# Eleven operand instructions an item on GpSimd in place of VectorE, in a gated scan with two feed-forward layers

## The chip, the cores and the metric

The kernel runs on one core of one Trainium2 chip. The core has a matrix engine (PE, with its weight loads as PEld), a vector engine (VectorE, DVE), an activation engine (ScalarE, ACT), a general engine (GpSimd, POOL) and a queue that issues DMAs (SyncE, SP). Each works through its own list of instructions in order; they meet through semaphores. The metric is the time of one execution on the device in microseconds, as a median over runs.

## The reference

A gated scan over 6080 steps and two batches gives 12160 tokens of 256 values. Two feed-forward layers follow, each 256 to 2048 to 256, with different activations.

```python
sig = 1.0 / (1.0 + np.exp(-f_logit))
f = lower_bound + (1.0 - lower_bound) * sig
for t in range(S):                       # h, y: [B, 256]
    h = f[:, t] * h + (1 - f[:, t]) * x[:, t]
    y[:, t] = h
x = y.reshape(B * S, D)                  # 12160 x 256
h = x @ w_in1;  x = (h - np.tanh(h)) @ w_out1
h = x @ w_in2;  x = np.maximum(0.01 * h, h) @ w_out2
```

All is float32. The kernel keeps that precision by splitting each matmul operand in two parts, a high half that the matrix engine takes as it is (fp32r) and a low half, the rest: a product is then three matmuls, high x high, low x high and high x low.

## The kernel before, in words

**Items.** The tokens are cut in 12 blocks of 1024 (the last has 896), and a block passes through each layer as one *item*. The list of items alternates: item 0 and 1 are blocks 0 and 1 of layer one, then second-layer and first-layer items take turns (item 2 is block 0 of layer two, item 3 block 2 of layer one, and so on); from item 3 on, odd items are first-layer ones up to item 21, even items second-layer ones, and item 23 is the second-layer item of the last block. An item has 8 *units* of 256 of the 2048 inner values; a unit has four quarter steps (the calls of `work`).

**Products.** From item 3 on a unit computes its four 128 x 512 blocks c11, c12, c21, c22 by a scheme of seven products in place of eight (`product`), so it needs seven operands made of the four quarters of the token block: three quarters as they are (B11, B21, B22) and four differences, T1 to T4. Each has a high and a low half, in the tiles xh and xl of the item (two buffers of each, by `forms`). `make_forms` makes the jobs that write them: `split_hi` casts on ACT (line 570), `sub` takes a difference into a slot of the ring "t" (line 578), `split_lo` subtracts the high half from the value (line 574). The differences hang together: T2 is B22 minus T1, T4 is B21 minus T2. For a second-layer item the quarters come from the tile z, the result of layer one; for a first-layer item from y, the result of the scan.

**The rest of a unit.** ACT applies the activation (lines 658, 660); in layer one DVE subtracts it from the value (`shrink`, line 666); ACT casts the high half (`hi`, line 685) and DVE makes the low half (`lo`, line 690); `emit_B` (line 729) multiplies both by the second weight into four accumulator banks. Lines 1280 and 1324 on DVE add a copy (`s5`) to a PSUM bank of PE; line 1324 writes to an SBUF tile c22, line 1280 to the bank c12. Lines 779 and 791 join partial sums of the second-layer item before (`drain`, `combine`), line 824 transposes its output blocks, which SP then stores.

**What sets the order.** The order is written by hand: a table `side` says which jobs are called at which quarter step, and each job's instructions go to the end of its engine's list at the call. The operands of the next item are made during the item before it. In a first-layer item the jobs of the next second-layer item's operands come first, mixed with the output jobs of the item before, then the scan of the block for the next first-layer item:

```python
at = base + (10 if full else 6 if it == W0 - 1 else 4)
lay(base + 5, at, forms_in[:11 if full else 0])
rest_in = mix(forms_in[11 if full else 0:], outs)
```

`lay` spreads jobs over quarter steps by their weights; `base` is the first quarter step of the item, and `full` holds for items 7, 9, ... 21. So eleven of the eighteen jobs (six of them low halves and differences) are called within quarter steps 5 to 10. The order of the jobs there is: high halves of B11, B21, B22; low half of B11; T1; low half of B21; high half of T1; low half of B22; T3; low half of T1; high half of T3; then T2, low half of T3, high half of T2, T4, low half of T2, high half and low half of T4. In items 3 and 22 the jobs are spread over nearly the whole item, one or a few at a time.

Of the kernel before, what the change touches and what calls it, by code (L numbers as in the profile page):

```python
# [8 lines left out]
F32 = mybir.dt.float32  # L9
# [5 lines left out]
ALU = mybir.AluOpType  # L15
# [5 lines left out]
def tile_gated_scan_two_ffn(  # L21
# [23 lines left out]
    nc = tc.nc  # L45
# [15 lines left out]
    NPLAIN = 3  # L61
# [48 lines left out]
    def light(f, w=0.4):  # L110
        weight[f] = w
        return f
# [438 lines left out]
    def make_forms(it, spread=False):  # L551

        l, c = items[it]
        h = macros[c][1] // 2
        s = {}

        def q(k, n):
            if l == 0:
                return ys[c][:, k, n * h:(n + 1) * h]
            return zs[c][:, k, n, :h]  # L560

        def get(i):
            if i in s:
                return s[i][:, :h]
            return {B11: q(0, 0), B21: q(1, 0), B22: q(1, 1), B12: q(0, 1)}[i]

        def split_hi(i):
            if it not in forms:
                forms[it] = [xp.tile([P, 7, H], F32R, tag=f"x{v}", name=f"x{v}") for v in "hl"]
            nc.scalar.copy(forms[it][0][:, i, :h], get(i))  # L570

        def split_lo(i):
            hi, lo = forms[it]
            nc.vector.tensor_tensor(lo[:, i, :h], get(i), hi[:, i, :h].bitcast(F32), ALU.subtract)

        def sub(i, a, b):
            s[i] = sp.tile([P, H], F32, tag="t", bufs=6, name="t")
            nc.vector.tensor_tensor(s[i][:, :h], a(), b(), ALU.subtract)

        if it < NPLAIN:  # L580
            return [f for i in (B11, B21, B12, B22) for f in (
                lambda i=i: split_hi(i), lambda i=i: split_lo(i)
            )]
        jobs = []
        for i, make in (
            (B11, None), (B21, None), (B22, None),
            (T1, lambda: sub(T1, lambda: q(0, 1), lambda: q(0, 0))),
            (T3, lambda: sub(T3, lambda: q(1, 1), lambda: q(0, 1))),
            (T2, lambda: sub(T2, lambda: q(1, 1), lambda: get(T1))),
            (T4, lambda: sub(T4, lambda: q(1, 0), lambda: get(T2))),  # L590
        ):
            if make:
                jobs.append(make)
            jobs += [light(lambda i=i: split_hi(i)), lambda i=i: split_lo(i)]
        if spread:
            first = (0, 2, 4, 1, 6, 3, 7, 5, 9) if l else (0, 2, 1, 4, 3, 6, 5, 7, 9)
            jobs = [jobs[i] for i in first + (8, 10, 12, 11, 13, 15, 14, 16, 17)]
        return jobs
# [313 lines left out]
    with tc.manual_schedule():  # L912
# [105 lines left out]
        for u, (load, jobs, _) in enumerate(w):  # L1018
            a = begin[NU - 1] + 3 + 43 * u // 8
# [3 lines left out]
        a = 2 * I + 18  # L1023
# [54 lines left out]
        for it in range(2, len(items) - 1):  # L1078
            base = I * it
            l, c = items[it + 1]  # L1080
            if it in outer:
                f, w = make_forms(it + 1, True), crossing[it]
                a = 7 if l == 0 else 0
# [114 lines left out]
        for t in range(NPLAIN * NU, NC):  # L1198
# [4 lines left out]
            it, v = divmod(t, NU)  # L1203
            grp = []
            if it in outer and 2 <= v < crossing[it] + 2 or v < 2 and crossing.get(it - 1) == NU:
                a, w = (it, v) if v > 1 else (it - 1, v + NU)
                g, i = divmod(w - 2, 2)
                pairs[a, g] = us_of[a][2 * g:2 * g + 2]
                grp = [(a, g, 2 * i), (a, g, 2 * i + 1)]
            if t < NC:  # L1210
# [3 lines left out]
                b1, h = u["b1"], u["h"]  # L1214
# [102 lines left out]
            if it in outer and v < crossing[it]:  # L1317
                g, i = divmod(v, 2)
# [58 lines left out]
```

## Time and profile before

| | |
|---|---|
| median of 3 runs | 1936.88 us (1936.64 to 1938.4) |
| profiled execution | span 1935.1 us from its first to its last instruction; the median of the runs, which counts what lies around the span too, is 1.8 us more |
| PE busy | 1927.7 us, 100% by the page |
| DVE busy | 1748.6 us, 90% |
| ACT busy | 1496.7 us, 77% |
| POOL busy | 3.3 us, 11 instructions, the last before 19 us |
| PE clock | granted in full in all 40 slices |

The page's first part gives busy time by engine over the whole span. The table of stretches (`windows` of the trace) gives the same for parts of it, so it tells where an engine has room. The timeline gives instructions one by one with their start; a row can merge several of one kind, and then its duration is from the first's start to the last's end. Consecutive instructions of an engine overlap a little, so the spacing of starts is shorter than a duration.

### The profile page before, as it was taken

How to read it: one execution, taken by the hardware profiler on the slowest of the kernel's cores; microseconds unless marked ns; L12 is line 12 of the kernel's file. 1: busy time of each engine (PE TensorE's matmuls, PEld its weight loads, DVE VectorE, ACT ScalarE, POOL GpSimd, SP SyncE). 2: the span in 40 equal slices, each digit the busy share in tenths (PEclk: the TensorE clock that was granted, in tenths of full speed). 3: DMA queues.
4: the chain of work that ended last, by engine and by line, in shares of the span. 5: the costliest groups of instructions: out<-in, count | busy, mean ns of one | idle time of the engine just before them, and what ended most of it. 6: DMA issues, size and time to landing. Idle time of an engine off the chain costs nothing.

```text
span 1935.1 us, 26099 instructions
## 1 busy us (share of the span) xinstructions
PE 1927.7 (100%) x8606; PEld 1607.2 (83%) x8606; DVE 1748.6 (90%) x2848; ACT 1496.7 (77%) x2773; POOL 3.3 (0%) x11
## 2 busy tenths in 40 slices
PE   9999999999999999999999999999999999999999
PEld 7888888888888888888888888888888888889888
DVE  8989879878899988999999999999899999987997
ACT  7556656766698689689779769868968977976997
POOL 0000000000000000000000000000000000000000
PEclk9999999999999999999999999999999999999999
DMA  6668678987575757757567476575765756646665
GB/s 218 181 154 282 232 255 299 261 274 241 169 206 175 191 187 202 182 182 216 151 185 214 150 196 194 190 182 194 204 170 176 215 147 193 192 161 187 211 198 139
DMA packets 478214, 384.86 MB, mean 199 GB/s; under 512 B 280960, under 2 KB 367872, under 8 KB 478080
## 3 DMA queue, kind: packets, MB, share of 16 engines
q1 hardware_dynamic: 477568, 382.98, 66.0%
q8 instruction: 68, 1.11, 0.2%
q14 instruction: 66, 0.54, 0.1%
q10 hardware_dynamic: 512, 0.23, 0.0%
HBM read 341.31 MB, written 41.81 MB: 198 GB/s over the span
## 4 chain that ended last, share of the span: by engine, by line
PE 98%; DVE 1%; DMA 0%; issue 0%; ACT 0%; SPq 0%
PE acc L729 30%; PE b L606 23%; PE c L606 18%; PE acc L768 11%; PE acc L746 8%; PE b L628 5%; PE c L729 1%; PE c L628 1%; DMA rawx<-in_x_dram 0%; DVE g L666 0%; DVE gl L690 0%; PE b L636 0%; PE b L614 0%; DVE y L478 0%; SPq L445 0%
## 5 line engine op out<-in xcount | busy, mean ns | idle before, releaser
L729 PE MATMUL acc<-gh,wb 128*128 128x512 f32 (+1 forms) x1760 | 595.2, 387 | 0.0
L690 DVE TENSOR_TENSOR gl<-g,gh 128x512 fp32r<-128x512 f32 (+1 forms) x686 | 456.0, 678 | 36.4 <-ACT gh L685 31.3
L685 ACT CAST gh<-g 128x512 fp32r<-128x512 f32 (+1 forms) x686 | 411.6, 617 | 82.3 <-DVE g L666 79.1
L729 PEld LDWEIGHTS acc<-gh,wb 128*128 128x128 f32 x1760 | 330.4, 188 | 64.8
L729 PE MATMUL acc<-gl,wb 128*128 128x512 f32 (+1 forms) x880 | 340.6, 387 | 0.0
L606 PE MATMUL b<-xh,wy 128*128 128x512 f32 (+1 forms) x672 | 260.0, 387 | 0.0
L606 PE MATMUL c<-xh,wa 128*128 128x512 f32 (+1 forms) x672 | 232.9, 387 | 0.0
L606 PE MATMUL b<-xh,wa 128*128 128x512 f32 (+1 forms) x672 | 232.9, 387 | 0.0
L658 ACT ACTIVATE g<-c 128x512 f32<-128x512 f32 (+1 forms) x244 | 141.7, 602 | 112.2 <-PE c L606 95.2
L729 PEld LDWEIGHTS acc<-gl,wb 128*128 128x128 f32 x880 | 165.2, 188 | 32.4
L660 ACT ACTIVATE g<-c 128x512 f32<-128x512 f32 (+1 forms) x272 | 155.6, 607 | 39.1 <-PE c L606 32.4
L746 PE MATMUL acc<-gh,wb 128*128 128x512 f32 (+1 forms) x468 | 168.7, 388 | 0.0
L666 DVE TENSOR_TENSOR g<-c,g 128x512 f32<-128x512 f32 (+1 forms) x243 | 157.0, 673 | 6.4 <-ACT g L658 6.2
L1324 DVE TENSOR_TENSOR c<-b,s 128x512 f32<-128x512 f32 (+1 forms) x168 | 113.9, 678 | 48.3 <-PE b L606 47.0
L606 PEld LDWEIGHTS b<-xh,wa 128*128 128x128 f32 x672 | 126.2, 188 | 24.7
L606 PEld LDWEIGHTS c<-xh,wa 128*128 128x128 f32 x672 | 126.1, 188 | 24.7
L606 PEld LDWEIGHTS b<-xh,wy 128*128 128x128 f32 x672 | 126.2, 188 | 24.6
L658 ACT ACTIVATE g<-b 128x512 f32<-128x512 f32 (+1 forms) x140 | 83.4, 596 | 66.3 <-PE b L628 59.8
L1218 ACT COPY c<-b 128x512 f32<-128x512 f32 (+1 forms) x168 | 96.5, 575 | 44.4 <-PE b L606 44.3
L606 PE MATMUL b<-xl,wy 128*128 128x512 f32 (+1 forms) x336 | 130.0, 387 | 0.0
L606 PE MATMUL b<-xl,wa 128*128 128x512 f32 (+1 forms) x336 | 130.0, 387 | 0.0
L606 PE MATMUL c<-xl,wa 128*128 128x512 f32 (+1 forms) x336 | 130.0, 387 | 0.0
(168 smaller groups left out, 3561.4 us busy)
## 6 DMA issues: line engine op xcount, KB each, us to landing
wa<-wa SPq DMA_DIRECT2D x189, 512.0 KB, 4.5
wy<-wa SPq DMA_DIRECT2D x168, 384.0 KB, 3.6
wb<-wb SPq DMA_DIRECT2D x112, 512.0 KB, 5.4
wg<-ws SPq DMA_DIRECT2D x117, 256.0 KB, 3.8
wb<-wb SPq DMA_DIRECT2D x78, 256.0 KB, 4.2
wa<-st SPq DMA_DIRECT2D x24, 512.0 KB, 3.6
out_dram<-o SPq DMA_DIRECT2D x176, 64.0 KB, 2.6
wb<-ws SPq DMA_DIRECT2D x78, 128.0 KB, 4.0
```

What stands on the lines that cost most here:

```text
L606: nc.tensor.matmul(bank[:, :h], wt[:, s, w], xx[:, v, :h], start=start and i == 0, stop=i == 2, skip_group_check=True,)
L628: nc.tensor.matmul(bank[:, :h], wt[:, s, 2 * k + j], xx[:, v[k], :h], start=i == 0, stop=i == 5,)
L658: nc.scalar.activation(g[:, :h], src[:, :h], AF.Tanh)
L660: nc.scalar.activation(g[:, :h], src[:, :h], AF.Prelu, alpha=0.01)
L666: nc.vector.tensor_tensor(g[:, :h], u["src", name][:, :h], g[:, :h], ALU.subtract)
L685: nc.scalar.copy(gh[:, :h], u["g", name][:, :h])
L690: nc.vector.tensor_tensor(gl[:, :h], u["g", name][:, :h], u["hi", name][:, :h].bitcast(F32), ALU.subtract)
L729: nc.tensor.matmul(bank[e][:, :h], w[:, j, s, es], v[:, :h], start=first and i == 0, stop=i == 2, skip_group_check=True,)
L746: nc.tensor.matmul(bank[:, :h], w[:, j, s, es], v[:, :h], start=first and i == 0, stop=i == 2, skip_group_check=True,)
L768: nc.tensor.matmul(bank[:, :h], w[:, v, s], x[:, :h], start=g == 0 and v == 0 and k == 0, stop=k == 2, skip_group_check=True,)
L1218: nc.scalar.copy(c11[:, :h], b1[:, :h])
L1324: nc.vector.tensor_tensor(c22[:, :h], b1[:, :h], s5[:, :h], ALU.add)
```

## The change

The low halves and the differences of second-layer operands are issued on GpSimd (`nc.gpsimd`) in place of VectorE (`nc.vector`). `l` is the layer of the item that the operands are for, `it` its number; item 2, whose operands are only low halves (`NPLAIN` is 3), stays as it was, and so do all first-layer operands. So the operands of items 4, 6, ... 22 and 23 are concerned. Those of item 23 are made in item 22, a second-layer one; all others in first-layer items.

```diff
         def split_lo(i):
             hi, lo = forms[it]
-            nc.vector.tensor_tensor(lo[:, i, :h], get(i), hi[:, i, :h].bitcast(F32), ALU.subtract)
+            eng = nc.gpsimd if l and it > NPLAIN else nc.vector
+            eng.tensor_tensor(lo[:, i, :h], get(i), hi[:, i, :h].bitcast(F32), ALU.subtract)
 
         def sub(i, a, b):
             s[i] = sp.tile([P, H], F32, tag="t", bufs=6, name="t")
-            nc.vector.tensor_tensor(s[i][:, :h], a(), b(), ALU.subtract)
+            (nc.gpsimd if l else nc.vector).tensor_tensor(s[i][:, :h], a(), b(), ALU.subtract)
```

The lists of PE, ACT and SP keep their order (with one line more in the file, line numbers behind 573 grow by one: 574 becomes 575, 578 becomes 579, 690 becomes 691). On DVE, 33 low halves of z, 44 low halves of t and 44 differences leave the list.

Here is DVE's list in the second and third unit of item 9, before (xl and xh are the low and high operands, t a difference, gl and gh the halves behind the activation, c_7796 the SBUF tile c22 of this unit, cross a partial sum of the item before):

```order
L779 TENSOR_TENSOR cross<-acc_92,cross 128x512
L690 TENSOR_TENSOR gl<-g,gh 128x512
L578 TENSOR_TENSOR t<-z 128x512
L1324 TENSOR_TENSOR c_7796<-b_86,s_7748 128x512
L574 TENSOR_TENSOR xl<-z,xh 128x512 x2
L791 TENSOR_TENSOR cross<-cross 128x512
L666 TENSOR_TENSOR g<-c_88,g 128x512
L666 TENSOR_TENSOR g<-c_7796,g 128x512
L578 TENSOR_TENSOR t<-z 128x512
L791 TENSOR_TENSOR cross<-cross 128x512
L666 TENSOR_TENSOR g<-b_86,g 128x512
L690 TENSOR_TENSOR gl<-g,gh 128x512 x2
```

And the same place of DVE's list with the change:

```order
L780 TENSOR_TENSOR cross<-acc_92,cross 128x512
L691 TENSOR_TENSOR gl<-g,gh 128x512
L1325 TENSOR_TENSOR c_7796<-b_86,s_7748 128x512
L792 TENSOR_TENSOR cross<-cross 128x512
L667 TENSOR_TENSOR g<-c_88,g 128x512
L667 TENSOR_TENSOR g<-c_7796,g 128x512
L792 TENSOR_TENSOR cross<-cross 128x512
L667 TENSOR_TENSOR g<-b_86,g 128x512
L691 TENSOR_TENSOR gl<-g,gh 128x512 x2
```

Two differences and two low halves are gone from between the others, which keep their order.

POOL's list for the operands made in item 9, with the change (before, POOL had nothing behind its two copies at the start of the kernel):

```order
L575 TENSOR_TENSOR xl<-z,xh 128x512
L579 TENSOR_TENSOR t<-z 128x512
L575 TENSOR_TENSOR xl<-z,xh 128x512 x2
L579 TENSOR_TENSOR t<-z 128x512
L575 TENSOR_TENSOR xl<-t,xh 128x512
L579 TENSOR_TENSOR t<-z,t 128x512
L575 TENSOR_TENSOR xl<-t,xh 128x512
L579 TENSOR_TENSOR t<-z,t 128x512
L575 TENSOR_TENSOR xl<-t,xh 128x512 x2
```

The eleven instructions stand in one list of their own, with nothing of other work between them.

## Rows read from the trace of the kernel before

**Rows 1.** Page, part 1: busy us (share of the span) xinstructions of each engine.

```profile
PE 1927.7 (100%) x8606; PEld 1607.2 (83%) x8606; DVE 1748.6 (90%) x2848; ACT 1496.7 (77%) x2773; POOL 3.3 (0%) x11
```

**Rows 2.** Table of stretches: start:end, length, then busy us of each engine.

```profile
0.00:279.57 279.57, 276.65 (x1246) 227.60 (x1247) 247.81 (x371) 174.11 (x300) 3.33 (x11) 1.00 0.68 221
279.57:1851.41 1571.84, 1571.84 (x6970) 1307.72 (x6969) 1432.77 (x2357) 1255.45 (x2337) 0.00 (x0) 1.00 0.67 197
1851.41:1935.10 83.69, 79.16 (x392) 71.89 (x390) 67.97 (x122) 67.14 (x137) 0.00 (x0) 0.99 0.58 169
```

**Rows 3.** Table of stretches, same columns: items 5, 7, 19 and 21.

```profile
441.49:523.09 81.60, 81.60 (x361) 67.57 (x360) 74.46 (x125) 55.18 (x98) 0.00 (x0) 1.00 0.68 194
597.27:680.91 83.64, 83.64 (x370) 69.28 (x369) 79.58 (x134) 58.97 (x108) 0.00 (x0) 1.00 0.58 164
...
1544.33:1627.97 83.64, 83.64 (x370) 69.28 (x369) 78.79 (x132) 58.57 (x108) 0.00 (x0) 1.00 0.58 162
...
1702.07:1777.89 75.82, 75.82 (x370) 69.31 (x369) 62.55 (x109) 50.39 (x100) 0.00 (x0) 1.00 0.54 164
```

**Rows 4.** Timeline of DVE in item 9: start us, duration us, line, tiles.

```profile
770.10 0.69 DVE L574 TENSOR_TENSOR xl<-z,xh 128x512 fp32r<-128x512 f32 x1 [1.28 <-ACT xh L570]
...
772.25 0.68 DVE L690 TENSOR_TENSOR gl<-g,gh 128x512 fp32r<-128x512 f32 x1
...
773.45 0.68 DVE L690 TENSOR_TENSOR gl<-g,gh 128x512 fp32r<-128x512 f32 x1
...
776.45 0.69 DVE L791 TENSOR_TENSOR cross<-cross 128x512 f32<-128x512 f32 x1
777.05 1.28 DVE L666 TENSOR_TENSOR g<-c,g 128x512 f32<-128x512 f32 x2
...
780.06 1.28 DVE L690 TENSOR_TENSOR gl<-g,gh 128x512 fp32r<-128x512 f32 x2
...
781.86 0.68 DVE L791 TENSOR_TENSOR cross<-cross 128x512 f32<-128x512 f32 x1
782.46 0.69 DVE L1280 TENSOR_TENSOR c<-b,s 128x512 f32<-128x512 f32 x1
```

**Rows 5.** Timeline of PE in the same item, same columns.

```profile
781.84 0.39 PE L729 MATMUL acc<-gl,wb 128*128 128x512 f32 x1
...
784.33 0.39 PE L606 MATMUL b<-xh,wy 128*128 128x512 f32 x1
```

**Rows 6.** Groups by line and shape, DVE: busy us, mean ns, idle before.

```profile
L578 DVE TENSOR_TENSOR t<-z 128x512 f32<-128x512 f32 x20 | 13.7, 685 | 0.0
```

**Rows 7.** Timeline of POOL, its three tensor_scalars.

```profile
1.37 0.53 POOL L928 TENSOR_SCALAR minus<-ident 128x128 f32<-128x128 f32 x1
4.47 0.31 POOL L942 TENSOR_SCALAR ga<-lb 128x2 f32<-128x2 f32 x1 [2.57 <-DMA lb<-in_lower_bound_dram]
4.75 0.19 POOL L943 TENSOR_SCALAR gb<-lb 128x2 f32<-128x2 f32 x1
```

**Rows 8.** Timeline of ACT in item 9, casts of second-layer operands.

```profile
769.45 1.66 ACT L570 CAST xh<-z 128x512 fp32r<-128x512 f32 x3
...
775.91 0.60 ACT L570 CAST xh<-t 128x512 fp32r<-128x512 f32 x1
...
780.94 0.62 ACT L570 CAST xh<-t 128x512 fp32r<-128x512 f32 x1
...
788.41 0.62 ACT L570 CAST xh<-t 128x512 fp32r<-128x512 f32 x1
```

**Rows 9.** Timeline of POOL and of DVE around 17 and 18 us.

```profile
17.00 1.09 POOL L482 COPY carry<-y 128x1 f32<-128x1 f32 x1 [12.07 <-DVE y L478]
...
18.17 0.56 POOL L482 COPY carry<-y 128x1 f32<-128x1 f32 x1
...
16.85 1.26 DVE L478 TENSOR_TENSOR_SCAN y<-g,y,v 128x512 f32<-128x512 f32 x1
...
18.03 0.67 DVE L154 TENSOR_SCALAR b<-b 128x1024 f32<-128x1024 f32 x1
```

## The prediction

> **What bounds the kernel now.** I read the engine shares of the page first [rows 1]: PE is busy for 1927.7 of the 1935.1 us of the span, so 7.4 us is all that it ever waits. The table of stretches says where [rows 2]. Up to 279.57 us PE is idle for 279.57 - 276.65 = 2.9 us, behind 1851.41 for 83.69 - 79.16 = 4.5 us, and in the 1571.84 us between for none at all. The chain that ended last is 98% PE by the page. Every moved instruction makes operands inside that middle stretch (the last of them are made for the last item), so no time can be gained there: the change is free, or it makes PE wait.
>
> VectorE (DVE) is the next engine. In the first-layer items 7, 9, ... 19, seven of one shape, of which the first and the last but one stand in the rows, it is busy for 79.58 and 78.79 us of 83.64 [rows 3]. Its timeline in item 9 (which begins at 755.09) shows work almost without a gap from 770 us on, one instruction every 0.60 us though each lasts 0.68 (781.86 to 782.46) [rows 4]. So there DVE runs a little behind and PE has only small margins. Two of them: the first `lo` of the pair at 780.06 ends near 780.74, and PE's first matmul on such a low half starts at 781.84, a margin of 1.1 us; `L1280` ends at 782.46 + 0.69 = 783.15, and the matmul that adds to the PSUM bank it has read starts at 784.33, a margin of 1.18 us [rows 4, 5].
>
> **The change part by part.** By the program's order 11 instructions move for each of the second-layer items 4, 6, ... 22 and 23: four differences (L578) and seven low halves (L574), 121 in all. The rows give 685 ns for a difference [rows 6] and 0.69 us for a low half (770.10) [rows 4]; between others it costs DVE its pitch of 0.60 us. DVE loses 11 x 0.60 = 6.6 us of work in such an item, 121 x 0.60 = 73 us in the kernel. On the path to the end this is worth nothing by itself, since PE has no idle time for it to fill.
>
> *What GpSimd (POOL) pays.* No row of before shows a POOL tensor_tensor. The nearest are its tensor_scalars: 0.31 and 0.19 us for 128x2, 0.53 us for 128x128 [rows 7]. The slope from 0.31 to 0.53 is 0.22/126 = 1.75 ns a column, so 512 columns of one input take 0.53 + 384 x 1.75 ns = 1.2 us. The upper end: the slope from 0.19 (0.34/126 = 2.7 ns) with the columns of two inputs read one after the other, 0.19 + 2 x 512 x 2.7 ns = 3.0 us. The lower end is DVE's own 0.60 us pitch. I take 1.2, from the largest tile that POOL has in this trace. Eleven such are 13 us, and the item has 838.73 - 770 = 69 us left when the first can start, so POOL is never late with the operands themselves: even eleven of 3.0 us (33 us) fit before the next item, which is the first to read them.
>
> *The waits that the change adds.* ACT's casts of the differences (L570) now wait for POOL in place of DVE, and behind them in ACT's queue stand the activations that PE needs. POOL has a shorter queue than DVE: the first cast of a difference stands at 775.91 [rows 8], and POOL, starting at 770.1 behind the cast at 769.45, has that difference (its second instruction) ready near 772.5. Three output transposes on DVE wait for POOL to release slots of the "t" ring; they stand behind the burst walked through below, and the POOL instructions that they wait for have their inputs by 782 us or by the cast at 788.41, before the transposes' own turn. Both groups cost nothing, unless POOL instructions last 3 us. The SP queue issues the same DMAs in the same order.
>
> *The cost that I expect.* POOL and DVE get in each other's way when both read two tensors of SBUF. One place in this trace shows the two side by side: a POOL copy of one column starts at 17.00 and lasts 1.09 us, four times the 128x2 tensor_scalar, and ends at 18.09; a DVE scan of two SBUF operands runs from 16.85 to 18.11. The next such copy, at 18.17, lasts 0.56 and ends at 18.73, beside a DVE instruction that ends at 18.70 [rows 9]. I read this as POOL held until DVE has ended, and take it that DVE is held in the same way where POOL was first. That second half no row shows.
>
> The Trainium skill's page "SBUF — State Buffer", section "Who interferes with whom", says the same of both directions: a VectorE instruction with two SBUF inputs and a GpSimd instruction that reads SBUF exclude each other for the whole instruction, whichever comes first. The trace agrees for the direction that it has (1.09 us for one column).
>
> Now the walk through item 9 with 1.2 us for a POOL instruction and 0.60 for one of DVE. POOL's first starts at 770.1 and ends at 771.3. Its next eight follow without a wait for data: four need only what is there by 771.1, and the two low halves among the others that need the casts at 775.91 and 780.94 have them before their turn. DVE's list between 771.3 and 782.46, without the moved ones, holds eight instructions with two SBUF inputs: the two `lo` at 772.25 and 773.45, the second `L666` of 777.05 (it reads `c22` and `g`), the pair of `lo` at 780.06, and three `L791`, of which the first and the last stand in the rows [rows 4]. The others read a PSUM bank and fit beside POOL. If the two engines take turns, each of the eight waits for a POOL instruction, and a turn lasts 1.2 + 0.6 = 1.8 us. Eight turns end at 771.3 + 14.4 = 785.7 and `L1280` at 786.4, where PE wants it at 784.33: 2.1 us late. The `lo` at 780.06 is the sixth: 771.3 + 10.8 = 782.1 against 781.84, 0.3 late, which is part of the 2.1. Behind this burst POOL waits for the cast at 788.41, DVE has 0.60 us less to do for each instruction removed, and nothing more is late.
>
> Seven such items: 7 x 2.1 = 14.7 us. I add nothing for the others: in item 21 (448 columns) DVE is busy for 62.55 of 75.82 us, and item 5 has 7.1 us to spare [rows 3]; in items 3 and 22 the jobs are spread over the item, so that the instructions come singly, and one POOL instruction delays one of DVE by at most 1.2 us, about the margin. The sum is 1935.1 + 14.7 = 1949.8 us of span. The span of the profiled execution lies 1.8 us under the median of the runs (1936.88), so the forecast is 1951.6.
>
> The Trainium skill's page "GPSIMD Engine Reference", section "Performance versus the Vector engine", gives 4497 ns for a tensor_tensor of 2048 float32 columns; an estimate from it is a quarter, 1.12 us. By that the item would be 9 x 0.08 = 0.7 us less late, and the sum 1946.6. No run here shows that figure yet.
>
> **How steep it is.** Nine POOL instructions stand before `L1280`'s turn ends, so an item is 2.1 + 9 x (p - 1.2) us late for a POOL time p. Nothing is late below p = 0.97; p = 1.5 makes 4.8 us an item and 1970.5; p = 3.0 would make 18.3 us an item and 2065, if POOL still took its turns.
>
> **The rivals.**
> *Nothing is late (not slower).* If POOL, once it meets DVE, always yields, or the two can read at once, DVE only loses work: the 11 instructions leave its busiest 30 us with 6.6 us of room, and PE goes on without a gap. The point from which this decides is 0.97 us a turn of POOL. For it: POOL has 69 us to do 13 us of work, and the only rows of the two side by side have POOL as the one that waited [rows 9]. Against it: those rows also show that the engines do exclude each other, and DVE has as many two-input instructions as others in the burst. Time: 1936.9, within 1 us.
> *POOL is much slower than 1.2 us.* Two inputs instead of one speak for it; the rows of [rows 7] are all of one input. From p = 1.5 on the time is over 1970.
> *Faster.* PE would have to lose over 3.9 of its 7.4 us of idle time. 2.9 of it lie before any moved instruction, and the 4.5 at the end lie in the closing products, whose operands DVE makes as before. At best some tenths come back; at most 1933.
> *The change doesn't do what it says.* The order shows the instructions gone from DVE and present on POOL, so I leave it at one in a hundred.
>
> **How the numbers follow.** Turns with about 1.2 us: 0.55, forecast 1951.6, its own range 1941 to 1970. Nothing late: 0.31, 1936.9. POOL at 1.5 us and more: 0.10. Faster: 0.03. No effect at all: 0.01. A measurement of this kernel can tell about 0.2%, or 3.9 us, from no change. Of the first case 0.05 falls within that bound (p near 1.0). So faster is 0.03, same 0.31 + 0.01 + 0.05 = 0.37, slower 0.50 + 0.10 = 0.60. For 8 times in 10 the range must take in the rival without a loss: 1936 to 1971, which leaves out the slow POOL and a part of the runs just under 1936.9.
>
> **What would show it.** Right: POOL rows of L575 and L579 near 1.2 us, longer where DVE is busy; `lo`, `L792` and the second `L667` of a pair in items 7 to 19 that last 1 to 2 us in place of 0.68 or start late without a releaser; and idle time of PE before the low-half matmuls and before the matmuls that wait for `L1281`, about 2 us an item near 15 us after its start. Wrong: DVE instructions still at 0.68 us beside POOL, and a PE that is busy for all 1571.84 us of the middle. If POOL's rows are near 2 us, the step that failed is its price; if they are near 1.2 and DVE's keep their length, it is the step that lets POOL hold DVE.

## The result and the profile after

The changed kernel takes 1951.85 us (median of 3 runs, 1951.68 to 1953.53) against 1936.88: a ratio of 1.0078 (95% interval 1.0062 to 1.0095). It is slower by 0.8%, and the forecast was 1951.6. The total came out as predicted; the way it is put together did not, as the rest shows. The profiled execution is the slowest of the three (1953.53 us), so the losses read from its trace add up to 16.6 us, where the medians differ by 15.0.

The page of the changed kernel, part 1 (columns as in [rows 1]) and the first line of part 4, the shares of the chain that ended last:

```profile
PE 1935.8 (99%) x8606; PEld 1604.8 (82%) x8606; DVE 1745.0 (89%) x2727; ACT 1500.2 (77%) x2773; POOL 186.8 (10%) x132
...
PE 75%; ACT 16%; DVE 7%; issue 1%; DMA 1%; SPq 0%; ACTq 0%; DVEq 0%
```

POOL has its 121 instructions more and DVE its 121 fewer, but DVE's busy time has fallen only from 1748.6 [rows 1] to 1745.0 us. The prediction counted 121 x 0.60 = 73 us as taken away; the run named fill only, below, measures 62. The chain, which was 98% PE before, now runs over DVE and ACT too.

The table of stretches, with the columns of [rows 2]: the middle stretch (items 3 to 22), then items 5, 21 and 22, each from PE's first operand matmul of the item to that of the next.

```profile
279.65:1868.19 1588.54, 1580.55 (x6971) 1305.91 (x6970) 1429.32 (x2236) 1258.81 (x2337) 183.55 (x121) 1.00 0.66 195
441.60:529.81 88.21, 83.80 (x362) 68.55 (x360) 76.54 (x114) 54.92 (x98) 16.10 (x11) 0.98 0.64 182
...
1712.86:1790.35 77.49, 76.76 (x370) 68.98 (x369) 61.73 (x98) 50.46 (x100) 16.89 (x11) 1.00 0.53 160
1790.35:1868.19 77.84, 75.52 (x329) 60.84 (x328) 68.94 (x99) 69.91 (x133) 15.77 (x11) 1.00 0.61 191
```

The middle stretch is 1588.54 long in place of 1571.84 [rows 2]: 16.7 us, which is the whole difference of the two spans (1951.7 - 1935.1 = 16.6). Item by item, against [rows 3]: item 5 takes 88.21 in place of 81.60, 6.6 more; the seven items 7, 9, ... 19 are 0.54 to 0.64 longer each (together 4.05, 0.58 on average); item 21 takes 77.49 in place of 75.82, 1.67 more; item 22 takes 77.84 against 73.52 before, 4.3 more. 6.6 + 4.05 + 1.67 + 4.3 = 16.6. Items 5, 21 and 22 carry three quarters of the loss, and the prediction gave them nothing. Item 3, to which it gave nothing either, lost 0.03.

Three groups of DVE by line and shape (busy us, mean ns of one | idle before):

```profile
L691 DVE TENSOR_TENSOR gl<-g,gh 128x512 fp32r<-128x512 f32 x628 | 447.5, 725 | 32.4 <-ACT gh L686 28.2 <-PE b L629 0.3
L1281 DVE TENSOR_TENSOR c<-b,s 128x512 f32<-128x512 f32 x152 | 105.2, 692 | 19.2 <-PE b L607 15.4 <-ACT g L661 1.0 <-ACT s L1266 0.5
L792 DVE TENSOR_TENSOR cross<-cross 128x512 f32<-128x512 f32 x27 | 31.2, 1156 | 0.0
```

`L792` reads two SBUF tensors and stands in the thick of the operands: its mean is 1156 ns, where the two in [rows 4] lasted 0.69 and 0.68 us. `L691` reads two as well, but most of its 628 are far from any POOL instruction, so its mean rises only a little. `L1281` reads PSUM and stays at 692. A POOL instruction takes 1.28 to 1.30 us where nothing holds it, as the next rows show.

The timeline of the changed kernel in item 9, which now begins at 762.49: POOL first, then DVE and one matmul of PE (start, duration, line, tiles, [idle before <- releaser]).

```profile
777.57 1.30 POOL L575 TENSOR_TENSOR xl<-z,xh 128x512 fp32r<-128x512 f32 x1 [128.45 <-ACT xh L570]
778.82 1.29 POOL L579 TENSOR_TENSOR t<-z 128x512 f32<-128x512 f32 x1
780.07 3.44 POOL L575 TENSOR_TENSOR xl<-z,xh 128x512 fp32r<-128x512 f32 x2
783.47 1.74 POOL L579 TENSOR_TENSOR t<-z 128x512 f32<-128x512 f32 x1
...
786.87 1.75 POOL L579 TENSOR_TENSOR t<-z,t 128x512 f32<-128x512 f32 x1
789.03 1.29 POOL L575 TENSOR_TENSOR xl<-t,xh 128x512 fp32r<-128x512 f32 x1 [0.41 <-ACT xh L570]
795.96 1.30 POOL L579 TENSOR_TENSOR t<-z,t 128x512 f32<-128x512 f32 x1 [5.63 <-DVE o L825]
```

```profile
779.67 0.99 DVE L691 TENSOR_TENSOR gl<-g,gh 128x512 fp32r<-128x512 f32 x1
781.19 1.18 DVE L691 TENSOR_TENSOR gl<-g,gh 128x512 fp32r<-128x512 f32 x1
782.89 1.17 DVE L792 TENSOR_TENSOR cross<-cross 128x512 f32<-128x512 f32 x1
783.99 1.78 DVE L667 TENSOR_TENSOR g<-c,g 128x512 f32<-128x512 f32 x2
785.69 1.78 DVE L792 TENSOR_TENSOR cross<-cross 128x512 f32<-128x512 f32 x1
787.99 2.89 DVE L691 TENSOR_TENSOR gl<-g,gh 128x512 fp32r<-128x512 f32 x2
791.40 0.69 DVE L1281 TENSOR_TENSOR c<-b,s 128x512 f32<-128x512 f32 x1
...
790.93 0.50 PE L730 MATMUL acc<-gl,wb 128*128 128x512 f32 x1
```

Read the starts against each other. POOL lasts 1.29 where DVE works on PSUM (778.82) and 1.74 where the two meet; DVE's 0.68 becomes 1.78 (785.69). Where both have two-input work, POOL starts every 1.70 us (783.47 to 785.18, which the dots leave out, then 786.87): one of POOL, one of DVE, in turns. The holds of DVE up to `L1281` add up to 0.31 + 0.50 + 0.49 + 0.50 + 1.10 + 1.61 = 4.5 us (a single lasts 0.68, a pair 1.28 [rows 4]). Six moved instructions are gone from before that place, 3.6 us. `L1281` starts 28.91 us into the item, where `L1280` started 782.46 - 755.09 = 27.37 [rows 4]: 1.54 late. The margin there was 1.18 [rows 5]. Yet little of PE's loss stands there. The held pair of `lo` (787.99, 2.89) ends at 790.88, and PE's matmul on its second low half starts right behind, at 790.93: the matmuls on that pair start 0.42 us late together, and the product that waits for `L1281`, pushed back by as much, adds under 0.1. With some hundredths at other matmuls item 9 loses 0.55, not 2.1.

The last difference, T4, did not follow. It waited 5.63 us for a transpose on DVE (`L825`): its slot of the ring "t" was still held by the output value `v` of item 8, which `out_of` takes from the same ring. So seven POOL instructions came in a row, an eighth 0.41 later, and the ninth fell behind `L1281`.

The same views in item 5 (begins at 441.60): DVE, POOL and PE of the timeline, then the table of stretches (the column behind POOL's is the granted clock).

```profile
460.09 1.69 DVE L691 TENSOR_TENSOR gl<-g,gh 128x512 fp32r<-128x512 f32 x1
461.70 2.93 DVE L330 TENSOR_TENSOR s<-f 128x256 f32<-128x256 f32 x2
464.55 1.49 DVE L330 TENSOR_TENSOR s<-s,f 128x256 f32<-128x256 f32 x1
465.96 2.26 DVE L667 TENSOR_TENSOR g<-c,g 128x512 f32<-128x512 f32 x2
468.15 1.78 DVE L337 TENSOR_TENSOR st<-s,st 128x512 fp32r<-128x512 f32 x1
...
461.19 3.16 POOL L575 TENSOR_TENSOR xl<-z,xh 128x512 fp32r<-128x512 f32 x2
...
466.70 0.50 PE L607 MATMUL c<-xh,wa 128*128 128x512 f32 x1 [2.50 <-DVE g L667]
471.18 0.50 PE L730 MATMUL acc<-gl,wb 128*128 128x512 f32 x1 [1.92 <-DVE gl L691]
```

```profile
464.00:468.00 4.00, 1.50 (x7) 1.08 (x7) 4.00 (x4) 2.65 (x5) 3.37 (x4) 1.00 0.47 166
468.00:471.00 3.00, 1.26 (x6) 0.72 (x4) 3.00 (x4) 2.04 (x4) 1.38 (x1) 1.00 0.07 26
...
472.50:475.50 3.00, 3.00 (x8) 2.32 (x8) 1.36 (x3) 1.24 (x2) 0.00 (x0) 0.50 0.92 296
```

In this item DVE also sums half-width pieces of a weight (`L330`, 128x256). They last 0.42 us when nothing holds them, and here three of them take 4.34: a short instruction waits for as long a POOL instruction as a long one does. Six DVE instructions are held one behind the other, PE loses 2.76 us at 466.70 and 2.22 at 471.18 (counted against the spacing of the same matmuls before; the first matmul behind a gap is 0.1 slower too), and then has its clock granted at 0.50, the 1.2 GHz level, from 472.5 to 475.5; its matmuls there start 0.42 to 0.43 us apart in place of 0.23. That takes another 1.6 us: 2.76 + 2.22 + 1.6 = 6.6.

And in item 22 (begins at 1790.35), DVE, then POOL and PE:

```profile
1807.16 1.65 DVE L691 TENSOR_TENSOR gl<-g,gh 128x512 fp32r<-128x512 f32 x1
1808.73 3.19 DVE L698 TENSOR_TENSOR t<-g 128x512 f32<-128x512 f32 x2
...
1808.22 1.59 POOL L579 TENSOR_TENSOR t<-z 128x448 f32<-128x448 f32 x1
...
1813.18 0.50 PE L747 MATMUL acc<-gl,wb 128*128 128x512 f32 x1 [1.27 <-DMA wg<-wb]
```

The operands of item 23 were to come "singly" here. They come in a three (from 1806.81) and in pairs later, because POOL has nothing else to do and starts all that its casts and slots allow, and DVE's list in a second-layer unit is one two-input instruction behind another, with little that reads PSUM between them. The three delay the `gl` at 1812.45 so that it ends at 1813.13, and PE's matmul on it starts at 1813.18. The row puts that gap down to a DMA; in the halves version below the same matmul has the same gap (1.28 us, at 1802.35), and the trace names `gl` there. The three cost PE 2.7 us, and of the later pairs two cost 0.75 each.

### The profile page after: what moved, and what is told of

It is laid out like the page before. It is cut to its first block, busy times and chain, and to the rows that moved or that the text cites. A ratio compares the mean times of both kernels' runs of the same rounds, so it can differ in the third digit from the quotient of the medians.

```text
span 1951.7 us, 26178 instructions
## 1 busy us (share of the span) xinstructions
PE 1935.8 (99%) x8606; PEld 1604.8 (82%) x8606; DVE 1745.0 (89%) x2727; ACT 1500.2 (77%) x2773; POOL 186.8 (10%) x132
## 4 chain that ended last, share of the span: by engine, by line
PE 75%; ACT 16%; DVE 7%; issue 1%; DMA 1%; SPq 0%; ACTq 0%; DVEq 0%
PE acc L730 26%; PE b L607 17%; PE c L607 13%; PE acc L769 6%; PE acc L747 5%; PE b L629 5%; ACT gh L686 3%; DVE gl L691 2%; ACT g L661 2%; ACT acc L784 2%; DVE g L667 2%; ACT cross L782 2%; PE c L730 1%; ACT xh L570 1%; ACT g L659 1%
## 5 line engine op out<-in xcount | busy, mean ns | idle before, releaser
L691 DVE TENSOR_TENSOR gl<-g,gh 128x512 fp32r<-128x512 f32 (+1 forms) x686 | 485.1, 720 | 36.4 <-ACT gh L686 31.5
L575 POOL TENSOR_TENSOR xl<-z,xh 128x512 fp32r<-128x512 f32 (+1 forms) x33 | 50.7, 1547 | 1456.2 <-ACT xh L570 1456.2
L667 DVE TENSOR_TENSOR g<-c,g 128x512 f32<-128x512 f32 (+1 forms) x243 | 168.6, 721 | 10.6 <-ACT g L659 10.4
L1325 DVE TENSOR_TENSOR c<-b,s 128x512 f32<-128x512 f32 (+1 forms) x168 | 114.1, 679 | 55.9 <-PE b L607 54.8
L1281 DVE TENSOR_TENSOR c<-b,s 128x512 f32<-128x512 f32 (+1 forms) x168 | 115.2, 686 | 25.6 <-PE b L607 17.0
L667 DVE TENSOR_TENSOR g<-b,g 128x512 f32<-128x512 f32 (+1 forms) x137 | 92.9, 678 | 43.3 <-ACT g L659 42.0
```

Of the source, the lines that this page charges most:

```text
L667: nc.vector.tensor_tensor(g[:, :h], u["src", name][:, :h], g[:, :h], ALU.subtract)
L691: nc.vector.tensor_tensor(gl[:, :h], u["g", name][:, :h], u["hi", name][:, :h].bitcast(F32), ALU.subtract)
L1281: nc.vector.tensor_tensor(c12[:, :h], b1[:, :h], s5[:, :h], ALU.add)
L1325: nc.vector.tensor_tensor(c22[:, :h], b1[:, :h], s5[:, :h], ALU.add)
```

## The experiments

The first four were timed beside runs of the kernel before at 1936.95 us, the last four beside runs at 1937.38. This table gives what each kernel's traces show: us lost against the kernel before in each item (items 7 to 19: the seven together), from the starts of PE's first matmul of each item. The time is the median, the items are those of the one profiled execution.

| kernel | time | item 5 | 7 to 19 | 21 | 22 |
|---|---|---|---|---|---|
| the change | 1951.85 | 6.61 | 4.05 | 1.67 | 4.32 |
| operands of 6 and 23 on DVE | 1942.84 | 0.00 | 3.60 | 1.68 | 0.02 |
| T4 without a slot | 1961.22 | 6.68 | 11.92 | 2.80 | 5.13 |
| fill only | 1937.09 | 0.00 | -0.01 | 0.00 | 0.01 |
| one input | 1937.93 | 0.05 | 0.00 | 0.03 | 0.95 |
| differences only | 1939.92 | 0.00 | 0.62 | 0.45 | 1.57 |
| low halves only | 1946.57 | 2.53 | 4.32 | 1.16 | 1.74 |
| operands of 6 only | 1943.07 | 6.65 | 0.02 | 0.01 | 0.01 |
| halves | 1944.79 | 0.88 | 1.10 | -0.01 | 4.26 |

In four of the profiled executions (operands of 6 and 23 on DVE, one input, low halves, halves) item 23 is 1.06 to 1.14 us longer as well. POOL does nothing there; the matmuls start 206.7 ns apart in place of 202.6 from some 20 us into the item on, with the clock granted at 1.00. What sets that pace stays open; it is no part of the losses of the items before it.

**Operands of items 6 and 23 left on VectorE.** They are the ones made in items 5 and 22.

```diff
-            eng = nc.gpsimd if l and it > NPLAIN else nc.vector
+            eng = nc.gpsimd if l and it > NPLAIN and it not in (6, 23) else nc.vector
...
-            (nc.gpsimd if l else nc.vector).tensor_tensor(s[i][:, :h], a(), b(), ALU.subtract)
+            (nc.gpsimd if l and it not in (6, 23) else nc.vector).tensor_tensor(s[i][:, :h], a(), b(), ALU.subtract)
```

> The operands of items 6 and 23 are made on DVE again, those of items 4, 8, ... 22 stay on POOL. The trace of the change puts 6.6 us of its loss into item 5, 4.3 into item 22, 1.7 into item 21 and 0.58 into each of items 7 to 19. If the loss sits where PE's gaps stand, this kernel takes 1951.85 - 10.9 = 1940.9 us, with items 5 and 22 back at 81.60 and 73.52. Rival, that each moved instruction costs about the same wherever it stands: 22 of 121 instructions go back, so 1951.85 - 2.7 = 1949.1.

1942.84 us, ratio 1.0029 (1.0018 to 1.0041). Items 5 and 22 are back at their old length, and the other items keep theirs. 22 of the 121 instructions make 9 of the 15 us (by the items, 10.9 of 16.6). The expected 1940.9 is 1.9 too low, since it took the losses of a trace from a median.

**T4 without a slot of the ring.** It is written over the quarter of z that it is made from, which nothing reads behind it.

```diff
-            s[i] = sp.tile([P, H], F32, tag="t", bufs=6, name="t")
+            s[i] = zs[c][:, 1, 0] if l and i == T4 else sp.tile([P, H], F32, tag="t", bufs=6, name="t")
```

> The fourth difference is written over its own quarter of z in place of a slot of the ring t, so that POOL no longer waits 5.6 us for an output transpose on DVE and has nine instructions in a row in place of seven. If the burst that I walked through was shorter only for this wait, L1281 comes one more POOL turn late: PE loses about 0.7 us more in each of items 7 to 19 and 21, so 1951.85 + 5 = 1957. Rival, that turns are not what delays DVE, or that the wait was no cover: no change, 1951.85, the items at +0.58 as before.

1961.22 us, ratio 1.0126 (1.0112 to 1.014): taking a wait away makes the kernel 9 us slower. The timeline of this kernel in item 9, of POOL, DVE and PE:

```profile
779.86 1.29 POOL L579 TENSOR_TENSOR t<-z 128x512 f32<-128x512 f32 x1
...
791.32 1.74 POOL L579 TENSOR_TENSOR z<-z,t 128x512 f32<-128x512 f32 x1
...
791.84 1.77 DVE L792 TENSOR_TENSOR cross<-cross 128x512 f32<-128x512 f32 x1
793.54 0.68 DVE L1281 TENSOR_TENSOR c<-b,s 128x512 f32<-128x512 f32 x1
...
794.28 0.50 PE L607 MATMUL b<-xh,wy 128*128 128x512 f32 x1 [0.88 <-DVE c L1281]
```

T4 now starts where the low half before it ends, meets `L792` and holds it for 1.1 us; `L1281` starts 793.54 - 763.50 = 30.04 us into its item, 2.67 later than before the change, and PE waits for it. Items 7 to 19 lose 1.62 to 1.95 each in place of 0.58. So the slot's wait had kept the ninth instruction out of the burst, and with the ninth in it the walk of the prediction (2.1 an item) is nearly what the chip does: from POOL's second instruction (779.86) to `L1281` (793.54) the eight turns take 13.7 us, 1.7 each, where the walk had 1.8. The direction came out as expected, the size did not (1957 expected, by 0.7 us more an item; it was 1.1 more).

**Fill only.** POOL writes zeros into the same tiles, in the same order of its list; the subtractions are left out. The edit is shown against the kernel before.

```diff
+            if l and it > NPLAIN:
+                nc.gpsimd.memset(lo[:, i, :h].bitcast(F32), 0.0)
+                return
             nc.vector.tensor_tensor(lo[:, i, :h], get(i), hi[:, i, :h].bitcast(F32), ALU.subtract)
...
+            if l:
+                nc.gpsimd.memset(s[i][:, :h], 0.0)
+                return
             nc.vector.tensor_tensor(s[i][:, :h], a(), b(), ALU.subtract)
```

> Leaves out the subtractions of the moved instructions: POOL fills the same 121 tiles with zeros, so it writes as much and reads nothing. If DVE is held by POOL's reads of SBUF, DVE's two-input instructions stay at 0.68 us and PE has no gaps: 1936.9 us. Rival 1, that writes hold DVE too: L792 and the second L667 of a pair over 0.9 us and 1941 or more. Rival 2, that the loss comes from the waits between POOL, ACT and DVE, most of which stay: near 1951.

1937.09 us, ratio 1.0000 (0.9991 to 1.0009). Page part 1 of this kernel, the group of its low halves on DVE, and one place in item 9 (begins at 755.31) where POOL and DVE work side by side:

```profile
PE 1927.3 (100%) x8606; PEld 1606.9 (83%) x8606; DVE 1686.5 (87%) x2727; ACT 1496.4 (77%) x2773; POOL 61.5 (3%) x132
```

```profile
L696 DVE TENSOR_TENSOR gl<-g,gh 128x512 fp32r<-128x512 f32 x628 | 421.2, 683 | 32.5 <-ACT gh L691 28.2 <-PE b L634 0.3
```

```profile
764.25 0.53 POOL L575 MEMSET xl<- 128x512 f32 x1
...
764.20 0.69 DVE L696 TENSOR_TENSOR gl<-g,gh 128x512 fp32r<-128x512 f32 x1
```

Instructions of POOL that only write hold nobody: `gl` lasts 683 ns on average and 0.69 us beside a memset, and no item moves. But the run is no pure test of rival 2. A memset reads nothing, so POOL doesn't wait for ACT's casts, and seven of its instructions in item 9 now stand 7 to 10 us after the item's start, where the subtractions began at 15. The waits of rival 2 are settled by the next run. This run also measures the holds. DVE has the same list here as in the changed kernel and is busy for 1686.5 us, there for 1745.0: it was held for 58.5 us, of which 16.6 reached PE.

**One input.** POOL copies one tensor of SBUF in place of subtracting two (the subtractions are left out; the edit is against the kernel before).

```diff
+            if l and it > NPLAIN:
+                nc.gpsimd.tensor_copy(lo[:, i, :h], hi[:, i, :h].bitcast(F32))
+                return
             nc.vector.tensor_tensor(lo[:, i, :h], get(i), hi[:, i, :h].bitcast(F32), ALU.subtract)
...
+            if l:
+                nc.gpsimd.tensor_copy(s[i][:, :h], a())
+                return
             nc.vector.tensor_tensor(s[i][:, :h], a(), b(), ALU.subtract)
```

> Leaves out the subtractions: POOL copies one tensor into each of the 121 tiles (the high half, or the first quarter of a difference). If any POOL read of SBUF holds DVE, DVE's two-input instructions are still late, by the length of a copy; an estimate from the 128x128 tensor_scalar is 0.6 to 1.2 us a copy against 1.28 measured for two inputs, so between a third and nearly all of the loss stays: 1941 to 1951. Rival, that only two-input POOL instructions hold DVE: 1936.9 with DVE rows at 0.68.

1937.93 us, ratio 1.0007 (0.9998 to 1.0015): the time can't be told from that of the kernel before, and it lies under the 1941 to 1951 that was expected if a single read holds DVE. Yet the rows show that it does. POOL's first copy in item 9, and a group of DVE:

```profile
770.29 0.62 POOL L575 CAST xl<-xh 128x512 fp32r<-128x512 f32 x1 [129.42 <-ACT xh L570]
...
L797 DVE TENSOR_TENSOR cross<-cross 128x512 f32<-128x512 f32 x27 | 21.7, 803 | 0.0
```

A read of one tensor holds DVE too (803 ns in place of 684, the mean before), but a copy is over in 0.62 us when alone, the longest `L797` lasts 1.09, and so short a turn is hidden nearly everywhere but in item 22 (0.95 us lost). The copies stand in POOL's list where the subtractions stood and still wait for ACT's casts, and items 7 to 19 lose nothing: so the waits between POOL, ACT and DVE, rival 2 of the run above, do not make the loss. What costs is neither the issue on POOL nor the writing nor the waits, but how long a POOL instruction that reads SBUF lasts.

**Differences only.** The low halves go back to VectorE.

```diff
-            eng = nc.gpsimd if l and it > NPLAIN else nc.vector
+            eng = nc.vector
```

> Only the four differences of an item go to GpSimd; its seven low halves are back on VectorE. Theory (what costs is a row of turns, seven in a row in item 9 of the changed kernel): T1, T3 and T2 can still follow each other, T4 waits for its slot, so a row has three turns of about 1.1 us lost each, 3.3 us, less the 4 x 0.6 = 2.4 us that VectorE is spared: 0.9 us, inside the margin of 1.18. Items 7 to 19 lose under 0.2 us each, item 5 one or two us, item 22 under one: 1939, GpSimd rows 1.3 to 1.75 us. Rival (the loss goes with the number of GpSimd instructions): 4/11 of the 15 us, 1942.3.

1939.92 us, ratio 1.0013 (1.0005 to 1.0022), near the 1939 of the theory, with item 5 (0.00, where one or two us were expected) too high in it and item 22 (1.57, where under one was) too low. The differences of the quarters need no cast, so of the four for item 6 two now run at 432 and 436, in item 4, and the other two at 453 and 456, ahead of the short instructions near 460.

**Low halves only.** The differences go back to VectorE.

```diff
-            (nc.gpsimd if l else nc.vector).tensor_tensor(s[i][:, :h], a(), b(), ALU.subtract)
+            nc.vector.tensor_tensor(s[i][:, :h], a(), b(), ALU.subtract)
```

> Only the seven low halves of an item go to GpSimd; its four differences are back on VectorE. Theory (rows of turns): the low halves of the three quarters can follow each other, those of T1 to T4 each wait for a cast on ScalarE, which itself waits for VectorE's difference, so they come singly. Items 7 to 19 lose under 0.3 us each, item 5 about 2 (three turns among its short instructions), items 21 and 22 1 to 2 together: 1941. Rival (the loss goes with the number of GpSimd instructions): 7/11 of the 15 us, 1946.5.

1946.57 us, ratio 1.005 (1.0036 to 1.0064). The theory's 1941 was wrong here, and the rival's 1946.5 is met, though not for its reason: the loss is not spread by number of instructions (item 5 loses 2.5, not 7/11 of 6.6), and the differences alone cost 2.5, not 5.4. What the theory missed is the other side of the balance: DVE keeps its differences. Before `L1281` in item 9 the holds are now 3.0 us, less than the 4.5 of the changed kernel, but only four of the instructions before it are gone from DVE, 2.4 us in place of 3.6. Holds less what is spared are 3.0 - 2.4 = 0.6 us against 4.5 - 3.6 = 0.9, and `L1281` starts 28.55 us into the item, 1.18 late against 1.54 (the other 0.6, the same in both, is spared time in which DVE then waits). That is just the margin, and PE loses only 0.17 there. The next rows, of DVE and PE in item 9, show where the rest stands:

```profile
791.14 0.68 DVE L1325 TENSOR_TENSOR c<-b,s 128x512 f32<-128x512 f32 x1
...
791.41 0.97 PE L607 MATMUL b<-xh,wa 128*128 128x512 f32 x2
```

The pair of matmuls takes 0.97 in place of 0.62 us: its second starts at 791.88, behind the end of `L1325`, and costs 0.35. Between `L1281` and `L1325` stands a difference (`L579`, at 789.94) that this kernel has back on DVE. So items 7 to 19 lose as much as with all eleven, at other matmuls. The stretches of PE's clock in item 5 of this kernel:

```profile
464.00:468.00 4.00, 3.05 (x13) 1.93 (x11) 4.00 (x6) 4.00 (x8) 1.52 (x1) 1.00 0.58 213
468.00:471.00 3.00, 2.06 (x10) 1.62 (x10) 3.00 (x6) 0.72 (x2) 0.00 (x0) 1.00 0.69 249
471.00:474.00 3.00, 3.00 (x15) 2.48 (x14) 2.73 (x6) 1.95 (x4) 0.00 (x0) 1.00 0.80 270
```

Here PE stalls twice for 1.1 us, is busy for 3.05 and 2.06 us of the two stretches, and keeps its full clock; in the changed kernel it was busy for 1.50 and 1.26 of them, and the clock fell to half.

**Operands of item 6 only.**

```diff
-            eng = nc.gpsimd if l and it > NPLAIN else nc.vector
+            eng = nc.gpsimd if l and it == 6 else nc.vector
...
-            (nc.gpsimd if l else nc.vector).tensor_tensor(s[i][:, :h], a(), b(), ALU.subtract)
+            (nc.gpsimd if l and it == 6 else nc.vector).tensor_tensor(s[i][:, :h], a(), b(), ALU.subtract)
```

> Only the operands of item 6, which are made in item 5, are on GpSimd: eleven instructions of the 121. Theory (each item's loss is its own, and item 5's is the largest because its short VectorE instructions each wait for a whole GpSimd one): the 6.6 us of item 5 alone, 1943.5, with PE's granted clock again near half for some 3 us behind its two stalls. Rival (the losses are alike in all items, 15 us over 11 items): 1938.3.

1943.07 us, ratio 1.003 (1.0018 to 1.0041). Item 5 loses 6.65 and no other item anything: the losses are each item's own. The clock is granted at 0.52 in the same three us behind the two stalls. Eleven instructions, 9% of those moved, make 40% of the loss.

**Halves.** Each POOL instruction is cut in two of half the columns.

```diff
+            cuts = [slice(0, h // 2), slice(h // 2, h)] if l and it > NPLAIN else [slice(0, h)]
             eng = nc.gpsimd if l and it > NPLAIN else nc.vector
-            eng.tensor_tensor(lo[:, i, :h], get(i), hi[:, i, :h].bitcast(F32), ALU.subtract)
+            for k in cuts:
+                eng.tensor_tensor(lo[:, i, k], get(i)[:, k], hi[:, i, k].bitcast(F32), ALU.subtract)
```

and the same for the differences.

> Every GpSimd instruction of the change is cut into two of half the columns (256, or 224): the same work on the same tensors in 242 instructions. Theory (a VectorE instruction with two SBUF inputs waits for the one GpSimd instruction that is running): a GpSimd instruction lasts about 0.7 us and a turn takes 1.1 to 1.2 in place of 1.7, so each VectorE instruction loses 0.5 in place of 1.1. Items 7 to 19 lose nothing, item 5 one to two us, items 21 and 22 one to two together: 1940. Rival (what counts is the total time for which GpSimd reads): the loss stays, 1951.9, or more by the fixed cost of 121 more instructions.

1944.79 us, ratio 1.0039 (1.0027 to 1.0052), between the theory (1940) and the rival. In item 5 the loss falls from 6.61 to 0.88, in items 7 to 19 from 4.05 to 1.10, in item 21 from 1.67 to none: there the theory holds in the main (it had nothing left in items 7 to 19). In item 22 it stays, 4.26 against 4.32. The timeline of DVE there:

```profile
1796.84 1.16 DVE L694 TENSOR_TENSOR gl<-g,gh 128x512 fp32r<-128x512 f32 x1
1797.92 2.23 DVE L701 TENSOR_TENSOR t<-g 128x512 f32<-128x512 f32 x2
1800.08 1.16 DVE L701 TENSOR_TENSOR t<-g,t 128x512 f32<-128x512 f32 x1
1801.15 1.14 DVE L694 TENSOR_TENSOR gl<-g,gh 128x512 fp32r<-128x512 f32 x1
1802.22 1.15 DVE L701 TENSOR_TENSOR t<-g,t 128x512 f32<-128x512 f32 x1
```

Each half instruction of POOL (224 columns here) holds DVE for 0.47 us in place of 0.96, but there are twice as many, and DVE's next instruction always reads two SBUF tensors: six holds of 0.47 make the same 2.8 us as three of 0.96. I read the other items so (no run isolates it): only where DVE's list has instructions that read PSUM or waits of its own between the two-input ones does a part of POOL's time fall beside them; there shorter turns help.

None of these kernels beats the kernel before, and none could by much: where POOL holds nobody (fill only) DVE is spared 62 us, and the time is that of before.

## Why the forecast held, step by step

**No time to gain.** Right. Fill only shows it: 62 us less work on DVE (the prediction's 73 counted 0.60 for each instruction; it was 0.51), PE as busy as before, ratio 1.0000.

**POOL's price, 1.2 us.** Nearly right: 1.28 to 1.30 us alone. The extension of the one-input slope held by luck as much as by reason, since a one-input copy of that size takes 0.62. The estimate of 1.12 us from the Trainium skill's page "GPSIMD Engine Reference", section "Performance versus the Vector engine", is 0.17 lower than the rows.

**They exclude each other and take turns.** Right, and now shown in both directions: POOL's 1.29 becomes 1.74 and DVE's 0.68 becomes 1.78 where the two meet, they alternate one by one, instructions that read PSUM on DVE (`L1281`, 692) or only write on POOL (fill only) are not touched, and a POOL instruction with a single SBUF input is enough (one input). The Trainium skill's page "SBUF — State Buffer", section "Who interferes with whom", states which instructions exclude each other, and the runs agree with it in each of these; that the two take turns is what the rows show. A turn takes 1.70 us, less than 1.29 + 0.60 = 1.89, so by the rows some 0.2 us of a turn is shared, and the exclusion doesn't last quite the whole instruction, as the prediction has it from the Trainium skill. The first rival, POOL that always yields, is out: DVE was held for 58.5 us.

**The added waits cost nothing.** Right for ACT's casts and for DVE's transposes, which wait nowhere for POOL in the trace of the changed kernel, but incomplete: I asked only who waits for POOL in the ring "t", not for whom POOL waits there.

**"Its next eight follow without a wait for data."** This step failed. Of the prediction's walk, seven come in a row, the eighth waits 0.41 us for a cast and the ninth 5.63 for a slot that an output value holds. With that wait removed an item loses 1.62 to 1.95: the walk's 2.1, with eight turns of 1.70 in place of 1.8 us. The prediction's own formula, with the measured 1.29 for a POOL instruction, would have given 2.1 + 9 x 0.09 = 2.9; a price that was too low and a turn taken as the plain sum of both made up for each other in part. With the wait it is 0.58, and the seven items cost 4.05 in place of 14.7. PE's gaps stand 27 to 29 us after the item's start, not "near 15 us", where the burst begins.

**"I add nothing for the others."** This failed by as much on the other side: 12.6 us. Item 5's spare of 7.1 us was read as a mean over the item; its burst stands beside the short weight sums, each of which waits a whole POOL instruction, and the 1.6 us of half clock behind the stalls is in no term. "The instructions come singly" in item 22 took the calls' places in the program for the times of their execution; an idle engine runs ahead of its neighbours until a cast or a slot stops it. In item 3, of which the same was said, nothing was lost (0.03). Item 21 lost 1.67 at a lower DVE load, by the same burst.

So 1951.6 was met by two errors of about 10.6 and 12.6 us that nearly cancel, which is luck. They leave 1.9 us between the sum (1949.8) and the span of the profiled execution (1951.7); the span of the median run is 1950.1. The mechanism and the sign were right; the split was not, and without the slot's wait, which the prediction didn't see, the same forecast would have met a kernel 9.4 us slower than this one.

**The steepness.** The prediction gave 9 us an item for each us of POOL time above 0.97. The one-input kernel (0.62 us) loses nothing in items 7 to 19, which agrees. In item 22 no such threshold shows: the one-input kernel loses 0.95 us there, and the halves as much as whole instructions.

## What to carry to other kernels

Before moving a two-input vector instruction to GpSimd, ask what VectorE runs at that moment: beside instructions that read PSUM it cost nothing here (`L1281`, 692 ns before and after), beside instructions that read two SBUF tensors each cost VectorE up to 1.1 us of its 1.29, and a short one there waited as long as a long one. Read the place from when the idle engine can start (its casts and slots), not from where the call stands, and look for bursts rather than at an item's mean load. Where the moved work relieves an engine that PE doesn't wait for, there is nothing to win against that.

## What was not expected of the hardware

- Removing a wait of 5.6 us on POOL made the kernel 9 us slower (T4 without a slot).
- Two stalls of PE of 2.8 and 2.2 us in item 5, with 2.6 us of matmuls between them, were followed by 3 us at a granted clock of 0.50: 1.6 us lost behind 5.0 us of stall. Two of 1.1 us at the same matmuls (low halves only) were not.
- Holds stand in no wait list. The trace books them as a longer DVE instruction or, in the chain, as "issue", so a releaser is not named; the mean of a two-input group against a PSUM-reading one shows them.
- Cut in two, a POOL instruction takes 1.43 to 1.44 us when nothing holds it (the pairs at 771.17 and 772.56 of the halves version, in item 9) against 1.28 to 1.30 in one: the cut costs 0.15 us.
